# Lightning attention and a four-expert layer: the first stretch written as one list of steps, w1 loaded between chunks, values of the third unit at other places

## The chip, the cores and the metric

The kernel runs on one core of a Trainium2 chip. A core has TensorE (PE, matmuls, with its weight loads PEld), VectorE (DVE), ScalarE (ACT), GpSimd (POOL) and SyncE (SP, which issues most DMAs). The metric is the device time of one execution in microseconds (us). The kernel before has a median of 1180.59 us over three runs (1180.34 to 1181.72).

## What is computed

A linear attention with decay over 4 batches, 8 heads, 768 tokens and head size 64 is followed by four experts, all of them applied to every token and mixed by normalised weights. All values are float32. Cut to what matters:

```python
for b in range(nb):                                   # blocks of 64 tokens
    intra = np.einsum('bhic,bhjc->bhij', qb, kb) * Dmask[None]
    intra = np.einsum('bhij,bhjd->bhid', intra, vb)
    inter = np.einsum('bhid,bhde->bhie', qb * lam_pow[None], kv_state)
    out[:, :, sl] = intra + inter
    kv_state = lam_block * kv_state + np.einsum('bhsd,bhse->bhde', kb * rev_pow, vb)
...
p = domain_probs / (domain_probs.sum(-1, keepdims=True) + 1e-09)
for e in range(E):                                    # x is 3072 x 512, w1 512 x 1024, w2 1024 x 512
    h = np.maximum(x @ w1[e], 0.0)
    out += p[:, e:e + 1] * (h @ w2[e])
```

## The kernel before, in words

**Tiling.** A chunk is 128 tokens of one batch, all 8 heads; a batch has 6 chunks (NCH). A group is 8 chunks, 1024 tokens, and there are three groups. The attention's output for a group lies turned in `xT` (L309). A unit is one pair of a group and an expert, 12 in all, numbered from 0.

**Products.** The expert products are made by a scheme of seven products in place of eight (M1 to M7) with sums of operand blocks beforehand: sums S of w1, sums T of x and of w2. Most first products (`first_product`, L883, matmul L905) are nested: each of the seven is itself made of seven, and its operands are four more sums of each side. Second products (`second_product`, L944, matmul L959) use w2's T sums. The product of group 0 with expert 0 is special: it is made straight after the attention by `direct_product` (L1301, matmul L1315), which has four quarters for each of M1 to M7; M6, M7 and M4 add up in banks of their own (`pc` in the profile).

**The first stretch (L1366 to L1410).** The attention of group 0 is three steps a chunk. `turn` (L549) multiplies k by its decay on GpSimd (`kd`, L520), transposes q and k on TensorE into two PSUM banks, and copies them out on ScalarE. `scores` (L572) multiplies q with k, and kd with v; then VectorE masks the scores and adds to the state, `middle` for the second half-block, `end` for the next chunk's state (L605 to L616), whose scaled copy GpSimd makes at L616. `values` (L622) adds the part from the state and the part from the scores, ScalarE copies the result to `xT` (L661), and VectorE adds the rest (L664, emitted one step later through `adds`). A loop over i calls turn of chunk i, scores of i - 1 and values of i - 2, all three on the pair of PSUM banks `pairs[n % 3]`; the table `between` (L1366) puts quarter products of M1, M2 and M5 at given i. In the same loop come w1's sums S1 to S4 of expert 0 on GpSimd (`sum_w1`, L352), the first own sums of x for product M1 of unit 0's nested product (`own_x`, L1217, on VectorE), the T1 sum of x (`x_sums`, L1338), and the loads: chunks 0 to 3 ahead of the loop (L408 to L412), chunk i + 4 at the end of step i, w1's A12, A21 and A22 after i = 0, 1 and 2. A11 is used by M1, A12 by M2, S1 = A21 + A22 by M5, S2 = S1 - A11 by M6, S3 = A11 - A21 by M7 and S4 = A12 - S2 by M3.

**After it** M5, M6, M7, M3 and M4 of that product follow (L1431 to L1446), a quarter at a time, with one background step (`rest`) and one `pump` a quarter. Then come the units, each with seven positions i of eight parts x (L1472 to L1551): a second product of this unit and a first product of the next, in turn.

**What sets the order.** Each engine and SyncE's queue work in program order. A counter `now` goes up by one a step. `pump` (L150) takes at most one item from the list `chores` when `now` has reached `free`, which grows by GpSimd's counted work; chores are the preparation of weights (`prepare_w2`, L242: load B12 and B22, a pause of 4, load B11, then T3, B21 and T1, T2, T4), the raw w1 of expert 1, and that expert's own operand sums (`mine`, L1415). Before a first product the chores are taken at once until its operands are made (L885). SyncE's loads of w2 for a second product (`feed2`, L929) wait for a buffer that an earlier second product frees, and what is queued behind them waits too. `bring_across` (L368) cuts a DRAM-to-DRAM rearrangement of q and k into pieces that `trickle` issues one at a time.

**Attention of the later groups** is cut into 24 steps (`attention`, L666: turn, scores, values of each chunk, always on banks s0 and s1), and one is taken at chosen parts of the units (L1547): at x = 5 of each i, and at x = 2 of i = 1, 3 and 5 except in units 0 and 3.

Of the kernel before, what the change touches and what calls it, by code (L numbers as in the profile page):

```python
# [12 lines left out]
ALU = mybir.AluOpType  # L13
AX = mybir.AxisListType
FP32 = mybir.dt.float32
# [7 lines left out]
def kernel(  # L23
# [384 lines left out]
    for n, names in ((0, "qk"), (1, "qk"), (0, "v"), (2, "qk"), (1, "v"), (3, "qk")):  # L408
        load(n, names)
    raw_w1(0, "A11")  # L410
    load(2, "v")
    load(3, "v")  # L412
# [30 lines left out]
    q_decay = consts.tile([P, NHP, BL], FP32, name="q_decay")  # L443
    for r in range(2):
        nc.vector.tensor_copy(out=q_decay[half[r], :, 0], in_=lam_bc[half[r], 4 * r:4 * r + 4])
    m = 1
    while m < BL:
        nc.vector.tensor_tensor(
            out=q_decay[:, :, m:2 * m], in0=q_decay[:, :, 0:m],
            in1=q_decay[:, :, m - 1:m].to_broadcast([P, NHP, m]), op=ALU.mult,  # L450
        )
        m *= 2
# [77 lines left out]

    def begin_state(n):
        if n % NCH == 0:
            states[n] = small("kv")[:].rearrange("p (x h d) -> p x h d", x=2, d=D)
            nc.vector.memset(states[n][:, 0], 0.0)

# [36 lines left out]
    def scores(n, tags):  # L572
# [3 lines left out]
        qT, kT = turned[n][0:2]  # L576
        kd, vn = nat.pop((n, "kd")), nat[n, "v"]
# [34 lines left out]
        def end():  # L612
            s = states[n + 1] = small("kv")[:].rearrange("p (x h d) -> p x h d", x=2, d=D)
            passed(nc.vector, s[:, 0], states[n][:, 1])
            tt(nc.vector, s[:, 0], s[:, 0], added[1], ALU.add)
            passed(nc.gpsimd, s[:, 1], s[:, 0])  # L616
# [48 lines left out]

    def attention(g):  # L666
# [21 lines left out]
        return steps  # L688
# [528 lines left out]
    def own_x(m, at_once=False):  # L1217
# [49 lines left out]
        late.append((now[0] + 8, lambda: (ready(), keep())))  # L1267
# [90 lines left out]
    def quarter_5(x):  # L1358
# [7 lines left out]
    between = {  # L1366
        4: (m1[0], m1[2]), 5: (m2[0], m2[2]), 6: (m1[1],), 7: (m1[3],), 8: (m2[1],),
        9: (m2[3], quarter_5(0), quarter_5(2)),
    }
    for i in range(CPG + 2):  # L1370
        if i == 6:
            chores.extend((*prepare_w2(0), *(raw[n] for n in ("A11", "A22", "A21"))))
        more = list(between.get(i, ()))
        order = [(turn, 0), (scores, 1), (values, 2)]
        if i == 3:
            order[0:2] = order[1::-1]
        for f, lag in order:
            n = i - lag
            if more and lag == 0 and i < CPG:
                more.pop(0)()  # L1380
            if 0 <= n < CPG:
                f(n, pairs[n % 3])
            if i < 2 and lag == 0:
                warm(3 - i)
            if i == 6 and lag == 2:
                sum_w1(0, "S1", "A21", "A22", ALU.add)
                sum_w1(0, "S3", "A11", "A21", ALU.subtract)
                own_blocks["M1"] = own_x("M1", True)
            if i == 7 and lag == 2:
                sum_w1(0, "S2", "S1", "A11", ALU.subtract)  # L1390
                sum_w1(0, "S4", "A12", "S2", ALU.subtract)
            if i == 8 and lag == 0:
                x_sums(("T1", 0))
            if i == 9 and lag == 2:
                x_sums(("T1", 1))
            if more and (lag == 2 or i >= CPG):
                more.pop(0)()
            now[0] += 1
            pump()
        while more:  # L1400
            more.pop(0)()
        if i + 4 < CPG:
            load(i + 4)
        if i < 3:
            for name in (("A12",), ("A21",), ("A22",))[i]:
                raw_w1(0, name)
        if i == 5:
            nc.scalar.dma_start(out=probs[:], in_=moe_domain_probs.rearrange("(t p) e -> p t e", p=P))
# [22 lines left out]
    for m in SEQ0[2:]:  # L1431
# [4 lines left out]
        for x, f in enumerate(work):  # L1436
            f()
            for y in sums_then.get((m, x), ()):
                y()
            rest()  # L1440
# [31 lines left out]
    for at, (g, e) in enumerate(units):  # L1472
# [14 lines left out]
        for i in range(7):  # L1487
# [34 lines left out]
            for x, part in enumerate(order):  # L1522
# [24 lines left out]
                if steps and (at > 0 or i > 1) and (x == 5 or (x == 2 and i in (1, 3, 5) and at not in (0, 3))):  # L1547
                    steps.pop(0)()
# [4 lines left out]
    assert not (background or aside or chores or queue or late or results)  # L1553
# [28 lines left out]
```

## Time and profile before

| what | value |
|---|---|
| median of three runs | 1180.59 us |
| the profiled execution, its span | 1180.84 us, 1179.1 us |
| TensorE busy | 1159.9 us, 98% |
| VectorE, ScalarE, GpSimd busy | 793.6, 272.5, 651.0 us |
| mean granted clock of TensorE | 0.997 |
| DMA | 324.45 MB, mean 275 GB/s |

Busy time is the union of an engine's instructions. A row of the timeline has start, length, engine, line, operation, output and inputs by the program's names, how many instructions were merged, and in brackets the idle time before the first with what ended it. "issue" stands for idle time in which the engine waited for nothing that the profile shows. PE clock 0.50 means that the chip granted half of TensorE's clock. A share of DMA is the mean busy share of 16 DMA engines.

### The profile page before, as it was taken

What the parts mean: (1) busy time and instruction counts of PE and PEld (TensorE: products, weight loads), DVE (VectorE), ACT (ScalarE), POOL (GpSimd) and SP (SyncE); (2) the same over time, 40 slices, a digit from 0 to 9 for tenths busy, and PEclk for the clock granted to TensorE, in tenths of its full rate; (3) what the DMA queues carried; (4) which work ended last, traced back from release to release, by engine and by line L of the source; (5) the groups of instructions that cost most, each with busy time, mean ns of one, the idle gap of its engine ahead of it and who ended that gap; (6) DMA issues with size and microseconds to landing.
All of it is one profiled execution on the core that took longest, in us unless ns stands there. A gap on an engine that the chain in (4) does not pass through costs nothing.

```text
span 1179.1 us, 21213 instructions
## 1 busy us (share of the span) xinstructions
PE 1159.9 (98%) x8159; PEld 1011.2 (86%) x8159; DVE 793.6 (67%) x1417; ACT 272.5 (23%) x500; POOL 651.0 (55%) x624
## 2 busy tenths in 40 slices
PE   7899999999999999999999999999999999999998
PEld 7788888888888888888888888888888888888887
DVE  5686796468467857747856764764665676777785
ACT  2323122112201211311220110121243342341231
POOL 2567348539548910065436655415683683783884
PEclk8999999999999999999999999999999999999999
DMA  8779799999999997899998899898986657566543
GB/s 203 191 238 279 252 298 341 366 324 338 351 363 337 318 292 232 260 312 294 326 306 274 280 308 313 283 321 289 315 283 244 248 199 280 196 251 236 214 165 86
DMA packets 265621, 324.45 MB, mean 275 GB/s; under 512 B 121488, under 2 KB 206896, under 8 KB 265520
## 3 DMA queue, kind: packets, MB, share of 16 engines
q1 hardware_dynamic: 254912, 320.27, 81.9%
q10 hardware_dynamic: 10608, 2.82, 1.1%
q8 instruction: 65, 1.06, 0.4%
q14 instruction: 36, 0.29, 0.1%
HBM read 237.69 MB, written 89.54 MB: 278 GB/s over the span
## 4 chain that ended last, share of the span: by engine, by line
PE 95%; DVE 3%; DMA 1%; SPq 1%; issue 0%; ACT 0%; ACTq 0%; DVEq 0%
PE pg L905 39%; PE q L959 33%; PE pq L1185 13%; PE pM L1315 2%; PE pc L1315 2%; PE op L638 1%; PE sp L585 1%; PE op L654 1%; DVE m L96 1%; PE sp L592 1%; PE qp L561 1%; PE kp L561 1%; DVE sums L96 0%; DMA vn<-in_v_dram 0%; DVE hS L96 0%; SPq L124 0%
## 5 line engine op out<-in xcount | busy, mean ns | idle before, releaser
L905 PE MATMUL pg<-xs_in,ws_in 128*128 128x256 f32 x1960 | 469.8, 380 | 0.3 <-DVE m L96 0.3
L905 PEld LDWEIGHTS pg<-xs_in,ws_in 128*128 128x128 f32 x1960 | 371.2, 190 | 52.2 <-DVE m L96 1.8
L96 DVE TENSOR_TENSOR m<-pg,m 128x512 f32<-128x512 f32 x451 | 307.2, 686 | 99.6 <-PE pg L905 93.2
L959 PE MATMUL q<-w2t,hS 128*128 128x256 f32 x1024 | 243.4, 380 | 0.0
L959 PEld LDWEIGHTS q<-w2t,hS 128*128 128x128 f32 x1024 | 193.2, 190 | 26.5
L975 DVE SCALAR_TENSOR_TENSOR acc<-q,gate,acc 128x256 f32<-128x256 f32 x192 | 92.5, 482 | 160.6 <-PE q L959 160.2
L959 PE MATMUL q<-w2t,m 128*128 128x256 f32 x768 | 182.7, 381 | 0.0
L959 PEld LDWEIGHTS q<-w2t,m 128*128 128x128 f32 x768 | 144.8, 190 | 19.9
L917 ACT ACTIVATE m<-m 128x512 f32<-128x512 f32 x132 | 83.0, 630 | 278.6 <-DVE m L96 277.3
L96 POOL TENSOR_TENSOR m<-m,xT 128x512 f32<-128x512 f32 x64 | 80.6, 1275 | 73.0 <-ACT m L917 55.4
L96 POOL TENSOR_TENSOR kv<-kv,q_decay 128x256 f32<-128x256 f32 x20 | 13.9, 696 | 161.9 <-DVE kv L96 132.9
L96 DVE TENSOR_TENSOR sums<-pq,sums 128x256 f32<-128x256 f32 x153 | 64.1, 421 | 46.1 <-PE pq L1185 38.9
L913 ACT COPY m<-pg 128x512 f32<-128x512 f32 x88 | 51.5, 585 | 172.2 <-PE pg L905 162.8
L1185 PE MATMUL pq<-acc,w2t 128*128 128x256 f32 x352 | 86.6, 379 | 0.0
L1185 PEld LDWEIGHTS pq<-acc,w2t 128*128 128x128 f32 x352 | 66.8, 190 | 9.3 <-issue 0.3
L96 POOL TENSOR_TENSOR acc<-hT,hT 128x512 f32<-128x512 f32 x32 | 40.2, 1271 | 30.3 <-PE pq L1185 28.4
L96 POOL TENSOR_TENSOR w2o<-w2b 128x512 f32<-128x512 f32 x32 | 40.4, 1283 | 26.9 <-DMA w2b<-in_moe_w_dram 25.1
L96 POOL TENSOR_TENSOR ops<-w2b 128x256 f32<-128x256 f32 x24 | 19.2, 820 | 62.1 <-DMA w2b<-in_moe_w_dram 54.7
L848 ACT ACTIVATE m<-m 128x512 f32<-128x512 f32 x44 | 27.7, 630 | 104.5 <-DVE m L96 104.5
L96 DVE TENSOR_TENSOR hS<-m,m 128x512 f32<-128x512 f32 x56 | 46.7, 836 | 5.0 <-ACT m L917 5.0
L96 DVE TENSOR_TENSOR m<-m,m 128x512 f32<-128x512 f32 x56 | 47.0, 839 | 0.0
L96 POOL TENSOR_TENSOR acc<-hT,acc 128x512 f32<-128x512 f32 x32 | 40.7, 1271 | 7.4 <-PE pq L1185 5.4
(165 smaller groups left out, 1376.7 us busy)
## 6 DMA issues: line engine op xcount, KB each, us to landing
xs_in<-x_ops SPq DMA_DIRECT2D x70, 896.0 KB, 6.5
ws_in<-w_ops SPq DMA_DIRECT2D x70, 896.0 KB, 8.5
w2t<-w_ops SPq DMA_DIRECT2D x66, 256.0 KB, 6.8
w2t<-w_sums SPq DMA_DIRECT2D x64, 256.0 KB, 3.9
w_ops<-ops SPq DMA_DIRECT2D x28, 512.0 KB, 5.6
w2t<-in_moe_w_dram SPq DMA_DIRECT2D x48, 256.0 KB, 4.1
w2b<-in_moe_w_dram SPq DMA_DIRECT2D x32, 256.0 KB, 5.8
w_sums<-w2o SPq DMA_DIRECT2D x16, 512.0 KB, 4.6
```

Source lines behind the costliest of these rows:

```text
L96: eng.tensor_tensor(out=o, in0=a, in1=b, op=op)
L561: nc.tensor.transpose(out=x[:, ac * C:(ac + 1) * C], in_=y[:, 2 * ac:2 * ac + 2].rearrange("p r d -> p (r d)"), identity=ident[:],)
L585: nc.tensor.matmul(out=sp[r][half[x], ac * BL:(ac + 1) * BL], lhsT=hc(kT)[half[r], ac, blk[x]], rhs=hc(qT)[half[r], ac, blk[x]], start=(ac ...
L592: nc.tensor.matmul(out=sp[x][half[r], 256 + ac * D:256 + (ac + 1) * D], lhsT=kd[half[x], 2 * ac + r], rhs=vn[half[x], 4 * r + ac], start=F ...
L848: nc.scalar.activation(out=o[:], in_=o[:], func=AF.Relu)
L905: nc.tensor.matmul(out=p[:, j * 256:(j + 1) * 256], lhsT=ws[i][:, j * P:(j + 1) * P], rhs=xs[i], start=(fresh and j == 0), stop=True, skip ...
L913: nc.scalar.copy(out=new[at][:], in_=p[:])
L917: nc.scalar.activation(out=new[at][:], in_=new[at][:], func=AF.Relu)
L959: nc.tensor.matmul(out=p[:, s * DH:(s + 1) * DH], lhsT=h[A_OF[m]][:, c * 256 + s * P:c * 256 + (s + 1) * P], rhs=fed2[g, e, m][uu][:, c], ...
L975: nc.vector.scalar_tensor_tensor(out=o, in0=x, scalar=w, in1=o, op0=ALU.mult, op1=ALU.add)
L1185: nc.tensor.matmul(out=p[:, 0:256], lhsT=fed3[e, m, x // 2][:, x % 2, c * P:(c + 1) * P], rhs=b[B_OF[i]][:, c * 256:(c + 1) * 256], start= ...
L1315: nc.tensor.matmul(out=p[:, s * 256:(s + 1) * 256], lhsT=a[c][:, f:f + P], rhs=b[:, c, j * 256:(j + 1) * 256], start=(s == 0 and c == 0 an ...
```

## The change

1. The loads ahead of the loop become q and k of chunks 0 and 1, v of 0 and 1, w1's A11, chunk 2, A12, chunk 3. The others follow in steps 3 to 6: chunks 4 and 5, 6, 7, and then A21 and A22.
2. `q_decay` is made by four scans over the block instead of six doubling products.
3. The scaled copy of the state that GpSimd makes moves from the end of `scores` into `begin_state`, which `turn` and now `scores` call: it is issued at the next chunk's turn, or at its scores if these were issued before the state was there.
4. The loop over i becomes a list of 34 steps. PSUM pairs are taken in turn by every call, not by chunk. The order from chunk 2 on has a quarter product between the scores and the values of most chunks.
5. S1 is issued with turn 7, S2 with the last quarter of M2, S3 behind M5's second remaining quarter, S4 behind M6's first. The own x sums of M1 are no longer made in the first stretch but by the chore `mine["M1"]`. The chores begin at step 30.
6. `m1[4]()` and `m2[4]()` are called twice. The first has no effect for M1; the second sets up M2's hidden block and appends its five background steps, so these are made twice.
7. The steps of the later attention have their places written out. For group 1, units 0 and 1 keep theirs; in the third unit turn and scores keep theirs too, and values move from (i, x) = (1, 5), (3, 5) and (5, 5) to (2, 2), (4, 2) and (6, 2). For group 2 nothing moves.

```diff
-    for n, names in ((0, "qk"), (1, "qk"), (0, "v"), (2, "qk"), (1, "v"), (3, "qk")):
+    for n, names in ((0, "qk"), (1, "qk"), (0, "v"), (1, "v")):
         load(n, names)
     raw_w1(0, "A11")
-    load(2, "v")
-    load(3, "v")
+    load(2)
+    raw_w1(0, "A12")
+    load(3)
...
+    lam_q = consts.tile([P, NHP], FP32, name="lam_q")
     for r in range(2):
-        nc.vector.tensor_copy(out=q_decay[half[r], :, 0], in_=lam_bc[half[r], 4 * r:4 * r + 4])
-    m = 1
-    while m < BL:
-        nc.vector.tensor_tensor(
...
+        nc.vector.tensor_copy(out=lam_q[half[r]], in_=lam_bc[half[r], 4 * r:4 * r + 4])
+    for ac in range(NHP):
+        nc.vector.tensor_tensor_scan(
...
     def begin_state(n):
-        if n % NCH == 0:
+        if n % NCH == 0 and n not in states:
...
+        if n % NCH and n in states and n not in carried:
+            carried.add(n)
+            passed(nc.gpsimd, states[n][:, 1], states[n][:, 0])
...
         qT, kT = turned[n][0:2]
+        begin_state(n)
...
-            passed(nc.gpsimd, s[:, 1], s[:, 0])
...
+    FEW = tuple((i, 5) for i in range(7))
+    MANY = (0, 5), (1, 2), (1, 5), (2, 5), (3, 2), (3, 5), (4, 5), (5, 2), (5, 5), (6, 5)
+    WIDE = (0, 5), (1, 2), (2, 2), (2, 5), (3, 2), (4, 2), (4, 5), (5, 2), (6, 2)
...
+    PLACES = {1: places(u0=FEW[2:], u1=MANY, u2=WIDE), 2: places(u3=FEW, u4=MANY, u5=MANY[:7])}
...
-    for i in range(CPG + 2):
...
+    pair = itertools.cycle(pairs)
+
+    def attend(f, n):
+        return lambda: f(n, next(pair))
+
+    ts, ss, vs = ([attend(f, n) for n in range(CPG)] for f in (turn, scores, values))
...
+    for f in (
+        (ts[0], lambda: warm(3)), (ts[1], lambda: warm(2)), (ss[0], loads(4, 5)), (ss[1], loads(6)), (vs[0], loads(7)),
+        (vs[1], loads("A21", "A22")), (ts[2],), (m1[0],), (ss[2],), (m1[2],), (vs[2],), (ts[3],), (m2[0],), (ss[3],), (m2[2],),
+        (ts[4],), (vs[3],), (ss[4],), (ts[5],), (m1[1],), (vs[4],), (ss[5],), (ts[6],), (m1[3],), (vs[5],), (ss[6],),
+        (ts[7], sum_first("S1", "A21", "A22", ALU.add), load_probs), (m2[1],), (vs[6], sum_x(0)), (begin_chores, ss[7]),
+        (m2[3], sum_first("S2", "S1", "A11")), (vs[7],), (quarter_5(0),), (sum_x(1), quarter_5(2)),
+    ):
+        for work in f:
+            work()
+        now[0] += 1
+        pump()
+    later_sums = {("M5", 1): sum_first("S3", "A11", "A21"), ("M6", 0): sum_first("S4", "A12", "S2")}
+    m1[4]()
+    m2[4]()
     m1[4]()
     m2[4]()
...
+            if (m, x) in later_sums:
+                later_sums.pop((m, x))()
...
-                if steps and (at > 0 or i > 1) and (x == 5 or (x == 2 and i in (1, 3, 5) and at not in (0, 3))):
-                    steps.pop(0)()
+                if steps and steps[0][0] == (at * 7 + i, x):
+                    steps.pop(0)[1]()
```

More of the change, by code (lines that the diff above doesn't have):

```diff
@@ L443 @@
     q_decay = consts.tile([P, NHP, BL], FP32, name="q_decay")
+    lam_q = consts.tile([P, NHP], FP32, name="lam_q")
     for r in range(2):
-        nc.vector.tensor_copy(out=q_decay[half[r], :, 0], in_=lam_bc[half[r], 4 * r:4 * r + 4])
-    m = 1
-    while m < BL:
-        nc.vector.tensor_tensor(
-            out=q_decay[:, :, m:2 * m], in0=q_decay[:, :, 0:m],
-            in1=q_decay[:, :, m - 1:m].to_broadcast([P, NHP, m]), op=ALU.mult,
+        nc.vector.tensor_copy(out=lam_q[half[r]], in_=lam_bc[half[r], 4 * r:4 * r + 4])
+    for ac in range(NHP):
+        nc.vector.tensor_tensor_scan(
+            out=q_decay[:, ac], data0=lam_q[:, ac:ac + 1].to_broadcast([P, BL]), data1=zeros[:, 0:BL],
+            initial=1.0, op0=ALU.mult, op1=ALU.add,
         )
-        m *= 2
     states = {}
@@ L529, in decayed @@
         tt(nc.gpsimd, *(x.rearrange("p (ac r) d -> p ac r d", r=2) for x in (kd, kn)), by, ALU.mult)
+    carried = set()
     def begin_state(n):
-        if n % NCH == 0:
+        if n % NCH == 0 and n not in states:
             states[n] = small("kv")[:].rearrange("p (x h d) -> p x h d", x=2, d=D)
             nc.vector.memset(states[n][:, 0], 0.0)
+        if n % NCH and n in states and n not in carried:
+            carried.add(n)
+            passed(nc.gpsimd, states[n][:, 1], states[n][:, 0])
     def turn_across(n):
@@ L664, in values, with places @@
             adds.append((now[0], lambda o=o, p=p: tt(nc.vector, o, o, p, ALU.add)))
+    FEW = tuple((i, 5) for i in range(7))
+    MANY = (0, 5), (1, 2), (1, 5), (2, 5), (3, 2), (3, 5), (4, 5), (5, 2), (5, 5), (6, 5)
+    WIDE = (0, 5), (1, 2), (2, 2), (2, 5), (3, 2), (4, 2), (4, 5), (5, 2), (6, 2)
+    def places(**units):
+        return [(int(at[1:]) * 7 + i, x) for at, of in units.items() for i, x in of]
+    PLACES = {1: places(u0=FEW[2:], u1=MANY, u2=WIDE), 2: places(u3=FEW, u4=MANY, u5=MANY[:7])}
     def attention(g):
@@ L687, in attention @@
             steps.append(end)
-        return steps
+        return list(zip(PLACES[g], steps, strict=True))
     hid = {}
@@ L1215, with own_x @@
     to_do, own_sums = {}, []
-    def own_x(m, at_once=False):
+    def own_x(m, at_once=False, wait=8):
         name = B_OF[m]
@@ L1266, in own_x @@
         keep = keep_own(("x", 0, m), x_ops[0, MS.index(m)], pieces)
-        late.append((now[0] + 8, lambda: (ready(), keep())))
+        late.append((now[0] + wait, lambda: (ready(), keep())))
         return {i: b[B_OF[i]] for i in B_OF}
@@ L1364, in quarter_5 @@
         return step
[L1366 to L1369, printed above, removed]
-    for i in range(CPG + 2):
[L1371 to L1408, printed above, removed]
@@ new lines, with sum_first, begin_chores, load_probs @@
+    pair = itertools.cycle(pairs)
+    def attend(f, n):
+        return lambda: f(n, next(pair))
+    ts, ss, vs = ([attend(f, n) for n in range(CPG)] for f in (turn, scores, values))
+    def sum_first(name, a, b, op=ALU.subtract):
+        return lambda: sum_w1(0, name, a, b, op)
+    def begin_chores():
+        chores.extend((*prepare_w2(0), *(raw[n] for n in ("A11", "A22", "A21"))))
+    def load_probs():
+        nc.scalar.dma_start(out=probs[:], in_=moe_domain_probs.rearrange("(t p) e -> p t e", p=P))
@@ new lines, in loads, with sum_x @@
+    def loads(*of):
+        return lambda: [raw_w1(0, x) if isinstance(x, str) else load(x) for x in of]
+    def sum_x(i):
+        return lambda: x_sums(("T1", i))
+    for f in (
[9 more added lines that the diff above has]
+        pump()
@@ L1552 @@
     pump(force=True)
-    assert not (background or aside or chores or queue or late or results)
+    assert not (later_sums or background or aside or chores or queue or late or results)
 _INS = ['q', 'k', 'v', 'lam', 'moe_domain_probs', 'moe_w1', 'moe_w2']
```

## The prediction, made before the change was run

> **What bounds the kernel now.** I read the busy table first, then the windows, then the timeline of TensorE, then its waits, then SyncE's and GpSimd's timelines where the moved steps meet them. The first line of the page settles what can be won:
>
> ```profile
> PE 1159.9 (98%) x8159; PEld 1011.2 (86%) x8159; DVE 793.6 (67%) x1417; ACT 272.5 (23%) x500; POOL 651.0 (55%) x624
> ```
>
> The span is 1179.1 us, so TensorE is idle for 19.2 us in all; the change removes none of its work, so it can win idle time and slow clock only. Where they lie is told by the windows (us of the span, then busy time of PE, PEld, DVE, ACT, POOL, granted clock, DMA share, GB/s):
>
> ```profile
> 5.70:16.42 10.72, 8.72 (x258) 7.75 (x258) 9.83 (x26) 4.38 (x9) 4.79 (x5) 1.00 1.07 246
> 16.42:23.25 6.83, 4.72 (x104) 4.30 (x104) 2.53 (x6) 1.17 (x2) 1.49 (x2) 0.50 0.80 191
> 23.25:41.40 18.15, 15.57 (x326) 13.49 (x320) 8.07 (x21) 6.31 (x14) 6.67 (x8) 1.00 0.91 221
> 41.40:66.20 24.80, 22.14 (x504) 18.55 (x502) 17.68 (x36) 8.08 (x18) 18.74 (x16) 1.00 0.55 159
> 66.20:94.00 27.80, 27.78 (x129) 24.46 (x130) 23.19 (x36) 10.20 (x18) 16.85 (x15) 1.00 0.90 268
> ```
>
> Up to 66.2, where product M6 starts (the `pc` rows), idle time is 2.00 + 2.11 + 2.58 + 2.66 = 9.35 us, and half of the 4.72 us at clock 0.50, 2.36 us, is lost too: **11.7 us** in reach there. TensorE's timeline (start, length, what, count, idle before and its releaser) has the causes:
>
> ```profile
> 14.31 0.62 PE L654 MATMUL op<-st,vn 64*64 64x64 f32 x27 [0.91 <-issue]
> 18.53 1.13 PE L592 MATMUL sp<-vn,kd 64*64 64x64 f32 x32 [3.07 <-DMA vn<-in_v_dram]
> 24.74 1.96 PE L1315 MATMUL pM<-xT,w1b 128*128 128x256 f32 x8 [1.31 <-ACT xT L661]
> 39.34 1.97 PE L1315 MATMUL pM<-xT,w1b 128*128 128x256 f32 x8 [1.27 <-DVE xT L96]
> 47.81 0.63 PE L561 MATMUL qp<-ident,qn 128*128 128x128 f32 x4 [1.69 <-issue]
> 62.09 3.69 PE L1315 MATMUL pM<-xt,w1o 128*128 128x256 f32 x16 [0.55 <-DVE xt L96]
> ```
>
> The longest is chunk 2's v, which stands behind w1's A11 and chunk 3's q and k; two are quarter products put directly behind the values they need. Later there are three idle times of 1.31 us, one per chunk of the third unit:
>
> ```profile
> 320.01 0.62 PE L638 MATMUL op<-qs,kv 64*64 64x64 f32 x26 [1.31 <-DVE kv L96]
> ```
>
> The others stand at 350.12 and 380.22: **3.93 us**. There values come three parts after scores and reuse the banks s0 and s1, which the state update still reads: the last DVE add (kv from sp, 379.75 to 380.17 for the third) ends just before TensorE goes on.
>
> [...] here these loads run at 191 to 246 GB/s, while 200 to 250 us shows 351. [...]
>
> **The order of the loads.** In KB from the start, v of chunk 2 ended at 3328 and landed at 18.40; it ends at 2816 now. The old landings (2560 KB at 15.08, 3072 at 17.37, 3584 at 20.51, 4096 at 22.58) give about 16.5 for it. In the new list it is due after turn 2 and one quarter, near 18.5: 3.07 goes. Chunk 3's k ends at 3840 KB, about 21.5, and is due at 22.3; A12 (3328, 18.4) is due at 23.3. w1's A21 and A22 now come last (8192 KB, landed at 41.36 before) and are used by GpSimd for S1. All these loads are new tiles, so SyncE should not wait for buffers. Cost nothing; if DMA is 1 us later, 0.2 to 1 us of it shows at turn 3.
>
> **The list of steps.** The same matmuls run. One by one from the old spacings, a turn takes 0.97 us, scores 0.98, values 1.05, a quarter 1.85. Old work from 5.69 to 66.22 is 60.53 - 11.7 = 48.8 us. What idles in the new list: (a) chunk 1's values need chunk 0's last state add, the GpSimd scaling (1.0) and a further DVE add: DVE 0.74 + 0.41 + 0.42 + 0.42 after the scores, then GpSimd, then 0.41; values 1 starts near 13.9 and TensorE idles 1.7. (b) Scores 4 follow turn 4 by one step only, and turn 4's ACT copies (0.59 each) queue behind the Relu of the quarter before, which waits for its DVE add (0.69): 0.8. (c) M6 behind the T2 sum: 0.44 as now. (d) Blocks of instructions: 2.60 now; the steps are spread more evenly, but follow one another faster; no row bounds it, so 0 to 2.6, taken as 1.0. Sum 3.9. M6 starts at 5.69 + 48.8 + 3.9 = 58.4 instead of 66.2: **-7.8**. The clock is taken as full: in the window from 13.0 to 16.4 TensorE is then busy some 60%, before 46%, and the window with the 1.27 us wait (63%) was not slowed. If it is slowed, 2.4 comes back. A quarter between scores and values (1.85) covers mask and state add (0.75 + 0.42); without it those 1.2 would show.
>
> **PSUM pairs in turn.** A pair is needed again three or more steps later, over 3 us, against ACT copies 0.65 and DVE adds 0.48: nothing. **q_decay**: six products with 2.96 us become four scans of 0.2 (eight took 1.57): DVE has q scaled 2 us sooner, hidden behind (a).
>
> **GpSimd's scaled state** moves from scores to the next turn, ahead of that chunk's kd. After scores: DVE 2.0, scaling 0.62, kd 1.06, together 3.7; TensorE has quarter, turn, values and half the next scores, 4.3: covered by 0.6. Behind turn 7 stand S1 and S2: about 46.7 + 2 x 2.7 = 52.1; the M5 quarters need S1 from 51. Just covered; each us later costs a us.
>
> **What moves behind M5 and M6.** S3 (2.7) and S4 (2.7) queue before T1, T2 of w2; S3 ends near 55, M7 needs it at 65. M1's own x sums leave DVE (44.69 to 47.3, 2.55 us) and come back as four subtractions (about 3.4) at unit 0's top, covered by the raw first block and the 1.73 us part ahead: 0.3. m2's end is called twice: the four S sums (0.67) and three ACT copies (0.58) of one hidden block are made twice, 2.7 us of DVE in M6 and M7. DVE has 0.44 us of gap per quarter after 80; M3's third quarter waits for its bank: 0.3.
>
> **The chores come later, and their DMAs.** They begin at slot 30 of 34 where it was 19 of 30, and w2's first pause ends in M5, not before. By the planner's count, the second expert's B21 load is issued two parts before product M5's operands are due; before, in unit 0's first part. Now (us, GpSimd, then SyncE):
>
> ```profile
> 99.91 2.50 POOL L96 TENSOR_TENSOR w2o<-w2b,w2o 128x512 f32<-128x512 f32 x2 [4.92 <-DMA w2b<-in_moe_w_dram]
> 102.48 1.41 POOL L96 TENSOR_TENSOR ops<-w1o 128x256 f32<-128x256 f32 x2
> ```
>
> ```profile
> 95.07 1.33 SPq L248 DMA_DIRECT2D w2b<-in_moe_w_dram  x2
> ```
>
> M5's first needed sum is ready at 103.2, TensorE needs it at 109.5: slack 6.3. GpSimd's chain S1, S2, S3, T3, S4, T1, T2 ends at 65.5 instead of 67.2, and the raw loads behind T2's store move by only -1.7; three more across transfers (0.8 each) stand ahead of B21: 95.7 issued, 100.5 landed, T4 2.5, first sum at 103.8. TensorE needs it at 58.4 + 27.7 (M6 to unit 0, as from 66.2 to 93.9) + 12.96 (one product pair, 7 x 0.86 + 4 x 1.73) + 2.6 (one part and a raw block) = 101.7: **+2.1**, between 0 and 5.
>
> **Third unit.** Values move from three to eight parts behind their scores; one part is 1.73 us: -3.93. What is late next: the sums of x for the third group begin 7.3 us later relative to the unit's end. M5's operand sums then end near 397.5, where their store stood at 396.7: about 0.8 of the slack is used, nothing shown.
>
> **Sum**: -7.8 - 3.9 + 0.3 + 0.3 + 2.1 = -9.0. The profiled execution took 1180.84 (span 1179.1 plus 1.74 around it), 0.25 above the median 1180.59. 1180.84 - 9.0 = 1171.8, for a median **1171.6**.
>
> **Rivals.** (B) Unit 0 doesn't wait and instruction blocks come in time: 1171.6 - 2.1 - 1.0 = 1168.5. For: SyncE's gates still hold slack. (C) The clock is halved again or blocks come late twice: + 2.4 to 3: 1174.3. For: the first chunks still leave 1.7 us of idle time. Against: no wait of 3 us is left. (D) The third unit's wait only changes its releaser: 1171.6 + 3.9 = 1175.5. Against: 5 parts, 8.6 us, for 1.31. (E) **Slower**: GpSimd falls behind at unit 0. Its products M5, M6 and M2 then each wait for a T or S sum (2.6) and four operand sums (3.0): 5.6 x 3 = 16.8 instead of 2.1, 1186.3. It decides from the point where GpSimd's first M5 sum comes some 12 us after 101.7. Against: GpSimd idles 6.7 us at 83 to 90 now. (F) The gain of the list is given back to the same DMA-bound start of the units, so that nothing moves: 1180.6.
>
> **Chances.** Forecast 0.45 (1169 to 1173.5), B 0.18, C 0.14, D 0.08, E 0.08, F 0.05, others faster 0.02. The range takes in B, C and D: 1167 to 1176.5. Faster by over 0.2% 0.87, the same 0.05, slower 0.08; 0.2%, 2.4 us, is about what a measurement of this kernel tells from no change.
>
> **What would show it.** M6 (`pc`) starting at 57 to 60 with clock 1.00 throughout; the 3.07 gone; a wait of about 1.7 near 13; none before `op<-qs,kv` around 310 to 380; a wait of some 2 us before `pg<-xt,ops` or `pg<-...w1o` near 101. It is wrong if M6 starts after 62, if S1 or S2 releases the M5 or M6 quarters, or if unit 0 shows waits on GpSimd in more than one product.

## The result and the profile after

The changed kernel takes **1187.45 us** (median of 6 runs, 1183.31 to 1187.85) against 1180.83 for the kernel before in the same comparison: a ratio of 1.0047, with a 95% interval of 1.0031 to 1.0063. It is slower by some 5.5 us by the ratio, and the medians lie 6.6 apart; 1171.6 was forecast. Its profiled execution took 1184.67 us (span 1182.8), 2.8 below its median; what the other runs lose beyond it, no profile shows.

TensorE's busy time rose by 3.1 us with the same number of matmuls, which is a first sign of lost clock:

```profile
PE 1163.0 (98%) x8159; PEld 1011.3 (86%) x8159; DVE 803.6 (68%) x1419; ACT 274.1 (23%) x503; POOL 648.5 (55%) x624
```

The windows of the changed kernel (us of the span, then busy time of PE, PEld, DVE, ACT, POOL, granted clock, DMA share, GB/s) show where: in 15.47 to 18.89 and in 411.42 to 418.25.

```profile
12.06:15.47 3.41, 1.38 (x75) 1.26 (x78) 2.69 (x7) 0.00 (x0) 1.09 (x2) 1.00 1.16 217
15.47:18.89 3.42, 3.42 (x75) 3.30 (x67) 0.97 (x4) 1.84 (x5) 1.20 (x2) 0.50 1.04 255
18.89:41.40 22.51, 22.01 (x513) 19.01 (x512) 13.04 (x32) 9.64 (x21) 6.22 (x7) 1.00 0.89 207
41.40:61.73 20.33, 18.37 (x380) 14.99 (x378) 12.55 (x26) 5.75 (x13) 14.81 (x12) 1.00 0.45 126
61.73:90.94 29.21, 28.11 (x129) 24.23 (x130) 26.62 (x40) 11.63 (x21) 17.72 (x15) 1.00 0.82 237
...
200.00:330.00 130.00, 130.00 (x1125) 112.59 (x1124) 83.46 (x142) 24.97 (x47) 76.21 (x77) 1.00 1.00 343
330.00:407.00 77.00, 75.75 (x584) 65.61 (x583) 63.02 (x104) 13.07 (x23) 59.52 (x60) 1.00 0.98 334
...
411.42:418.25 6.83, 6.07 (x14) 4.88 (x15) 0.00 (x0) 1.17 (x2) 6.44 (x9) 0.50 1.04 299
```

TensorE's timeline of the changed kernel, cut to rows ahead of which it idled (the bracket), and one row of the third unit:

```profile
15.01 0.50 PE L659 MATMUL op<-st,vn 64*64 64x64 f32 x17 [2.01 <-issue]
...
57.59 3.69 PE L1329 MATMUL pM<-xt,w1o 128*128 128x256 f32 x16 [0.58 <-DVE xt L96]
...
61.73 1.53 PE L1329 MATMUL pc<-xt,w1o 128*128 128x256 f32 x6 [0.44 <-DVE xt L96]
...
80.33 1.99 PE L1329 MATMUL pM<-xT,w1o 128*128 128x256 f32 x8 [1.10 <-DVE m L96]
...
107.50 1.13 PE L919 MATMUL pg<-xt,ops 128*128 128x256 f32 x4 [0.86 <-POOL ops L96]
...
138.21 1.10 PE L919 MATMUL pg<-ops 128*128 128x256 f32 x4 [0.96 <-DVE m L96]
...
164.50 1.13 PE L919 MATMUL pg<-xT,w1o 128*128 128x256 f32 x4 [1.02 <-DVE m L96]
...
326.77 0.69 PE L643 MATMUL op<-qs,kv 64*64 64x64 f32 x32
...
353.11 1.10 PE L919 MATMUL pg<-xs_in,ws_in 128*128 128x256 f32 x4 [1.25 <-DMA ws_in<-w_ops]
...
412.18 1.19 PE L919 MATMUL pg<-xs_in,ws_in 128*128 128x256 f32 x2 [3.17 <-DMA ws_in<-w_ops]
```

The wait of 3.07 for chunk 2's v is gone, and so are the three of 1.31: the row at 326.77 has no bracket. M6 (`pc`) starts at 61.73, not at 66.22. But waits stand now in units 0 and 1, and two for `ws_in`, the loaded operands of w1, later. A sum closes the account. The first `pg` matmul (`pg` is the bank of the nested first products, so this is where the units begin) starts at 92.66, where it was 95.65 (-2.99). Idle time after it is 8.17 us, where it was 4.88 (+3.29), and 6.83 us at half clock cost 3.41. Together +3.7, and the span grew from 1179.1 to 1182.8. (Without idle time and lost clock, the stretch from the first `pg` to the last matmul is 1074 to 1075 us in both, and within 1 us of that in nearly every run below.)

The chain of waits that ends at 412.18, in the changed kernel (start, length, what):

```profile
396.98 1.73 POOL xo L96
398.71 0.45 SPq L183
...
400.31 4.74 DMA x_ops<-xo
...
405.12 0.32 SPq L832
...
405.49 6.56 DMA ws_in<-w_ops
412.05 0.14 issue
412.18 1.19 PE pg L919 x2
```

GpSimd's sum of x, its store, the load of it and the load of `ws_in` behind that in SyncE's queue stand one behind another. In the kernel before, the same chain at that place holds matmuls only:

```profile
409.19 0.86 PE pg L905 x4
410.06 1.73 PE q L959 x8
411.78 1.29 PE pg L905 x6
```

There its load landed at 410.64 and was used at 411.62: 0.98 us to spare. That number was to be had before the prediction, and wasn't looked up.

### The profile page after: what moved, and what is told of

It is laid out like the page before. It is cut to its first block, busy times and chain, and to the rows that moved or that the text cites. A ratio compares the mean times of both kernels' runs of the same rounds, so it can differ in the third digit from the quotient of the medians.

```text
span 1182.8 us, 21229 instructions
## 1 busy us (share of the span) xinstructions
PE 1163.0 (98%) x8159; PEld 1011.3 (86%) x8159; DVE 803.6 (68%) x1419; ACT 274.1 (23%) x503; POOL 648.5 (55%) x624
## 2 busy tenths in 40 slices
DMA packets 265621, 324.45 MB, mean 274 GB/s; under 512 B 121488, under 2 KB 206896, under 8 KB 265520
## 3 DMA queue, kind: packets, MB, share of 16 engines
q8 instruction: 65, 1.06, 0.4%
## 4 chain that ended last, share of the span: by engine, by line
PE 88%; DVE 4%; DMA 4%; POOL 1%; issue 1%; SPq 1%; ACT 0%; ACTq 0%; DVEq 0%; POOLq 0%
PE pg L919 37%; PE q L973 30%; PE pq L1199 13%; PE pM L1329 2%; DMA ws_in<-w_ops 1%; DVE m L96 1%; PE op L643 1%; PE sp L591 1%; PE op L659 1%; PE sp L598 1%; DVE hS L96 1%; PE qp L566 1%; PE kp L566 1%; DVE xt L96 1%; PE pc L1329 1%
## 5 line engine op out<-in xcount | busy, mean ns | idle before, releaser
L96 DVE TENSOR_TENSOR m<-m,m 128x512 f32<-128x512 f32 x56 | 49.4, 882 | 0.0
L96 POOL TENSOR_TENSOR ops<-w1b 128x256 f32<-128x256 f32 x24 | 19.3, 823 | 43.4 <-PE pg L919 22.6
```

What stands on the lines that cost most here:

```text
L96: eng.tensor_tensor(out=o, in0=a, in1=b, op=op)
```

## The parts one by one

**The third unit alone.** The kernel before with the places of the third unit's values changed:

```diff
-if steps and (at > 0 or i > 1) and (x == 5 or (x == 2 and i in (1, 3, 5) and at not in (0, 3))):
+if steps and (at > 0 or i > 1) and (
+    x == 5 and not (at == 2 and i % 2)
+    or (x == 2 and i in (1, 3, 5) and at not in (0, 3)) or (x == 2 and i in (2, 4, 6) and at == 2)
+):
```

> The kernel before with one part of the change alone: values of the third unit at (2,2), (4,2), (6,2). Theory 1 (the later values themselves make the x sums of the third group late, and with them the first loads of the fourth unit): the three waits of 1.31 us go, but a wait of 2 us or more on xs_in or ws_in appears near 407 and TensorE's clock may be halved behind it, so 1179 to 1183 us, no gain. Theory 2 (the late chores of the new list are the cause, the values are harmless): 1180.8 - 3.9 = 1176.9 us, no wait near 407.

Measured 1178.2, ratio 0.9983 (0.9971 to 0.9994): about 2.0 of the 3.93 us, between what the two theories gave. The three waits are gone and none stands near 409, so later values by themselves don't make that wait. But two small ones came up behind them:

```profile
436.33 0.89 PE L905 MATMUL pg<-xs_in,ws_in 128*128 128x256 f32 x3 [0.62 <-DVE acc L975]
...
449.88 1.96 PE L905 MATMUL pg<-xs_in,ws_in 128*128 128x256 f32 x8 [0.36 <-DMA ws_in<-w_ops]
```

The first names VectorE, yet its `ws_in` landed at 436.19, 0.13 us ahead of the matmul. The load before 411 also lands 0.13 ahead, at 406.86. So several loads of this kernel land just in time, with nothing to spare.

**The third unit back, in the changed kernel.**

```diff
-PLACES = {1: places(u0=FEW[2:], u1=MANY, u2=WIDE), 2: places(u3=FEW, u4=MANY, u5=MANY[:7])}
+PLACES = {1: places(u0=FEW[2:], u1=MANY, u2=MANY[:9]), 2: places(u3=FEW, u4=MANY, u5=MANY[:7])}
```

> The changed kernel with the third unit's values back at (1,5), (3,5), (5,5). Theory 1: the wait of 3.17 us near 409 and the halved clock behind it (3.4 us) go, three waits of 1.31 us come back: 1187.4 - 6.6 + 3.9 = 1184.7 us, or less where the runs of 1187.4 lose more at that place than the profiled one of 1184.7. Theory 2: the wait near 409 stays, and 3.9 us are added: 1191 us.

Measured 1187.23, ratio 1.0065 (1.0047 to 1.0082), against 1187.45 and 1.0047 (1.0031 to 1.0063). In the profile the waits of 1.31, 1.37 and 1.90 are back and the two for `ws_in` are gone: waiting has moved from one place to another. The third unit's step gains 0.2 us here by the medians and 2.1 by the ratios, whose intervals overlap, so no gain of it is shown inside the changed kernel.

**Chores begun earlier, in the changed kernel.**

```diff
-(ss[5],), (ts[6],), (m1[3],)
+(ss[5],), (begin_chores, ts[6]), (m1[3],)
...
-(begin_chores, ss[7]),
+(ss[7],),
```

> The changed kernel with the chores begun at step 23 of 34 (11 steps ahead of M5's second half, as before) instead of step 30. Theory 2: the operands of units 0 to 3 come earlier, the waits at 106.6 (0.86), 351.9 (1.25) and 409.0 (3.17 and the halved clock, 3.4) go or shrink: 1178 to 1181 us. Theory 1: only the wait at 106.6 goes: 1186 us.

Measured 1181.42, ratio 1.0006 (0.9992 to 1.0019): some 5 us come back (4.8 by the ratios, 6.0 by the medians). No wait is left near 107, 137 and 164. But it is not faster than before, and what waits now is `ws_in`:

```profile
251.65 1.53 PE L919 MATMUL pg<-xs_in,ws_in 128*128 128x256 f32 x6 [2.15 <-DMA ws_in<-w_ops]
...
409.70 1.53 PE L919 MATMUL pg<-xs_in,ws_in 128*128 128x256 f32 x6 [1.00 <-DMA ws_in<-w_ops]
...
454.38 1.12 PE L919 MATMUL pg<-xs_in,ws_in 128*128 128x256 f32 x3 [3.01 <-DMA ws_in<-w_ops]
```

**Late chores alone, in the kernel before.**

```diff
-        if i == 6:
-            chores.extend((*prepare_w2(0), *(raw[n] for n in ("A11", "A22", "A21"))))
...
+            if i == 7 and lag == 1:
+                chores.extend((*prepare_w2(0), *(raw[n] for n in ("A11", "A22", "A21"))))
```

> The kernel before with one edit: the chores begin four steps of the planner later, at the scores of i = 7 and not at the top of i = 6. Nothing else of the change is in it. Theory 1 (it is the later chores that cost the changed kernel its gain): waits for GpSimd's operand sums near 107 to 112 of 0.8 to 2, waits of about 1 for DVE's own x subtractions near 140 and 167, and later ones for ws_in, together 3 to 6 us: 1183.5 to 1187. Rival (the later chores only cost together with the earlier M6, because GpSimd's sums keep their absolute time): M6 stays at 66.2, unit 0 shows at most 0.5 us of new waits, 1180 to 1182.

Measured 1184.39, ratio 1.0033 (1.0022 to 1.0043): +3.9 us from four planner steps (steps of the counter `now`), with M6 at 66.97 where it was 66.22. In the changed kernel the chores begin seven steps nearer to the end of the first stretch than before, so this is the smaller delay. Theory 1 holds in size; of the places that it named only the one near 140 came, with one later wait for `ws_in`, and no wait for GpSimd's sums:

```profile
140.82 1.10 PE L905 MATMUL pg<-ops 128*128 128x256 f32 x4 [0.96 <-DVE m L96]
...
458.02 1.32 PE L905 MATMUL pg<-xs_in,ws_in 128*128 128x256 f32 x5 [2.10 <-DMA ws_in<-w_ops]
```

What a wait on "DVE m" means here is seen in VectorE's timeline of the changed kernel ahead of 138.21: the chore that makes a product's own x sums is forced at the last moment, so four subtractions (the `ops` rows, 3.11 us) stand in one piece ahead of the sums (`m`) that empty the bank TensorE needs.

```profile
133.33 1.82 DVE L96 TENSOR_TENSOR ops<-xT 128x256 f32<-128x256 f32 x2
135.18 1.29 DVE L96 TENSOR_TENSOR ops<-xT,ops 128x256 f32<-128x256 f32 x2
...
136.78 0.68 DVE L96 TENSOR_TENSOR m<-m,m 128x512 f32<-128x512 f32 x1
137.38 1.28 DVE L96 TENSOR_TENSOR m<-pg,m 128x512 f32<-128x512 f32 x2
```

**Ends called once, in the changed kernel** (the second `m1[4]()` and `m2[4]()` deleted).

> The changed kernel with M1's and M2's ends called once each, so that M2's four S sums and three copies are made once. Theory that the doubled sums fill VectorE in M6 and M7: the wait of 1.10 us on VectorE at 79.2 goes, 1186.3 us, and unit 0 starts 1.1 us earlier. Rival (the time is lost at 352 and 409, where DMA is the limit): the 1.10 us are lost again there, 1187.4 us.

Measured 1183.95, ratio 1.0034 (1.0019 to 1.0049). The wait of 1.10 ahead of M3 is gone. That alone says little, since two other profiles with the ends called twice have no such wait over 0.3 either. A steadier measure is the time from M6 to the first `pg`: it is 29.43 us in all 14 profiles with the ends called once, the kernel before among them, and 30.94, 29.72, 30.41, 30.12 and 30.21 in the five with the ends called twice. So the doubled ends cost 0.29 to 1.51 us there. The total fell by more, but the intervals of this run and of the changed kernel overlap, and this run's profile is its longest (1192.91); more is not shown.

**The new order of loads alone, in the kernel before.**

```diff
-for n, names in ((0, "qk"), (1, "qk"), (0, "v"), (2, "qk"), (1, "v"), (3, "qk")):
+for n, names in ((0, "qk"), (1, "qk"), (0, "v"), (1, "v")):
...
-    load(2, "v")
-    load(3, "v")
+    load(2)
+    raw_w1(0, "A12")
+    load(3)
...
-        if i < 3:
-            for name in (("A12",), ("A21",), ("A22",))[i]:
-                raw_w1(0, name)
+        if i == 3:
+            raw_w1(0, "A21")
+            raw_w1(0, "A22")
```

> The kernel before with the new order of loads alone: v of chunk 2 ahead of w1's A12 and of chunk 3's q and k, and A21 and A22 after step 3; everything else is as before. Theory 1 (the 3.07 us wait for v was a matter of the order of the queue): the wait near 18 falls from 3.07 to under 0.8, the clock is not halved after it, so M6 starts 2.5 to 5 us before 66.2, at 61.5 to 63.7, and that gain reaches the end: 1175.5 to 1178.5 against some 1180.7. Theory 2 (the first stretch's loads are short of bandwidth as a whole, and another wait takes the place of this one): M6 at 65 or later, 1180 to 1182. Theory 3 (a gain there is given back by the units, whose loads don't come sooner): M6 at 61.5 to 63.7, but 1180 to 1182, with new waits for ws_in.

Measured 1181.82, ratio 0.9999 (0.9988 to 1.001), M6 at 66.92. Theory 2 holds: the wait for v becomes one for the q that now stands behind it.

```profile
13.36 1.09 PE L562 MATMUL qp<-ident,qn 128*128 128x128 f32 x4 [3.32 <-DMA qn<-in_q_dram]
```

So the new order gains nothing by itself. In the changed kernel the list takes turn 2 only after chunk 0's and 1's values; no run has the list with the old order, so what the order adds there is not shown.

**Four extra matmuls in TensorE's gap, in the changed kernel** (`lambda: warm(4)` ahead of `vs[0]`; their output isn't used).

> The kernel after with four extra matmuls of 128x128 on a constant, some 1.9 us, put in just before chunk 0's values; they fill time in which TensorE idles for 2.01 us by issue, and their output isn't used. Theory 1 (the idle time of that window halves the clock): the granted clock is 1.00 at 15.5 to 19, idle time before chunk 0's values falls by about 1, M6 starts 1.5 to 3 us earlier than 61.73. Rival (the wait is for a block of instructions, which begins at the same count of instructions wherever the idle time is, and the clock is halved by the idle time in sum): the 2.01 wait stays, moves behind the extra matmuls, the clock is still halved, M6 at 61.7 to 63.7. The total follows M6 only if the units don't give it back: 1184.5 to 1186 in the first case, 1187 to 1189 in the second, against 1187.4 of the kernel after.

Measured 1186.76, ratio 1.0044 (1.0029 to 1.0059). What the rival forecast came in this profile: the wait stayed at 1.99, moved behind the extra work, and the clock was halved at 16.3. The rows around the wait tell where it belongs. In the changed kernel it stands behind 14 of chunk 0's second group of matmuls:

```profile
12.57 0.43 PE L659 MATMUL op<-st,vn 64*64 64x64 f32 x14
15.01 0.50 PE L659 MATMUL op<-st,vn 64*64 64x64 f32 x17 [2.01 <-issue]
```

With the extra work, which shows as eight records, it stands eight records earlier in the program:

```profile
13.33 0.29 PE L659 MATMUL op<-st,vn 64*64 64x64 f32 x6
15.61 0.62 PE L659 MATMUL op<-st,vn 64*64 64x64 f32 x26 [1.99 <-issue]
```

In both, 220 matmuls come before it. So in these two profiles it belongs to a count of instructions and not to a place in the program (more on this in the last section). That it is a wait for a block of instructions, as the rival has it, is the author's reading; no row names what TensorE waits for.

One profile is too little for the clock, though. In the five profiles below that have the extra matmuls, this wait is 1.20 to 2.03 us and the clock behind it is not halved; in the five of the list without them it is 2.01 to 2.60 us and the clock is halved each time. So in these ten profiles the clock stayed where TensorE's idle time was filled (1.00 up to 63.22 us in the mended kernel, against 0.97 up to 61.70 in the changed one), as theory 1 had it. M6 starts no earlier for it: at 62.30 to 65.70 with the extra matmuls, at 61.73 to 64.79 without.

## What the mended kernel still waits for

**Early chores, ends once and the extra matmuls together**, with all of the change in it; then the same **with the third unit back** (`u2=MANY[:9]`), so that the list stands without the rest. (The run with early chores has the first, the run with four extra matmuls the last of these edits.)

> The kernel after with three edits together: the chores begin at step 23 as in the run with early chores, the ends of M1 and M2 are called once, and four extra matmuls fill TensorE's idle time before chunk 0's values. Theory 1 (chores, doubled end and halved clock are what the changed kernel lost, and they add up): 1181.4 of early chores, less 1.1 for M3's bank, less 1.5 to 3 for the clock: 1177 to 1179.5. Rival (the loads of the units start no sooner, so what the first stretch wins is waited for at ws_in): M6 at 60 to 62, waits for ws_in of 5 us or more between 200 and 460, 1180.5 to 1182.

> The mended kernel with the third unit's values back at their old places, so that the list of steps stands without the late chores, the doubled ends and the third unit's step; all loads are made. Theory (what the list wins up to unit 0, some 3 us, has only 1.84 us of slack at the fifth load of ws_in before it waits there): a wait of 0.7 to 2.5 near 248, with the clock halved behind it, the three waits of 1.31 are back, 1178.5 to 1182. Rival (the list's gain reaches the end if the third unit's step isn't made, and it was the two together that ran into DMA): no wait for ws_in, 1177 to 1178.

The mended kernel measured 1182.81, ratio 1.0015 (1.0002 to 1.0028), over 22 runs from 1176.72 to 1189.17. The list without the third unit's step: 1184.85, 1.0036 (1.0021 to 1.0051). Repairing what looked broken doesn't make the change win, and the list without the third unit's step is slower than the kernel before by some 4 us. The rival of the first holds (waits for loads of 5.6 in sum, though M6 is later than the 60 to 62 that it gave), and the second is worse than either theory gave. In the mended kernel M6 starts at 63.22 and the first `pg` 3.0 us earlier than before, and then:

```profile
250.34 2.14 PE L919 MATMUL pg<-xs_in,ws_in 128*128 128x256 f32 x7 [2.48 <-DMA ws_in<-w_ops]
...
409.30 1.97 PE L919 MATMUL pg<-xs_in,ws_in 128*128 128x256 f32 x8 [1.18 <-DMA ws_in<-w_ops]
...
438.74 1.53 PE L919 MATMUL pg<-xs_in,ws_in 128*128 128x256 f32 x6 [0.72 <-DMA ws_in<-w_ops]
```

When each `ws_in` landed and when its first matmul started (us; loads counted from the first, from the traces):

```
load        before            third alone       changed           mended
5th         248.77 / 250.61   248.99 / 250.62   248.17 / 251.36   250.25 / 250.34
11th        336.70 / 338.46   330.66 / 336.85   333.85 / 337.46   332.41 / 338.05
16th        410.64 / 411.62   406.86 / 406.99   412.05 / 412.18   409.17 / 409.30
19th        451.97 / 453.05   449.74 / 449.88   455.29 / 456.68   452.97 / 453.11
```

The 5th load lands at 248 to 250 whether TensorE comes early or not. Before, 1.84 us were to spare there and some 1 us at the 16th and 19th. A kernel that comes there 3 us earlier has to wait, unless the load moves too: with the third unit alone the 16th load lands 3.8 us earlier than before, and still only just in time. DMA is the busy resource: its share is 1.00 from 200 to 330 both before and in the changed kernel.

**Bytes or order?** Loads could also be late because of what stands ahead of them in SyncE's queue. To tell the two apart, some loads of `xs_in` (896 KB each) were to be left out. The first attempt, on the kernel before, on the third unit alone and on the mended kernel, left nothing out: its count (`len(fed)`) never took a value at which a load is skipped, and all 70 loads stand in the profiles.

> A control: the kernel before with less to load. Of the first 34 loads of x operands for the nested first products (xs_in) every second one is left out, and the product reads the x operands of the one before it, so its values are not those of the reference; the matmuls, their number and all other transfers stay. 17 transfers of 896 KB go, between 185 and 650 us. Theory (the kernel before waits for DMA nowhere in the units, but its nearest loads of ws_in land only 1 to 2 us ahead of use): nothing changes by more than 1 us, 1180 to 1181.5, while the slack of ws_in at 250 and 411 grows. Rival (DMA holds the kernel before back too): under 1179.

> The kernel before with the third unit's values later, and with the same 17 loads of xs_in left out as in the control (the same products read other x operands). Theory (alone, this step gained 2.5 where it removes 3.93 of waits, since loads of ws_in then land 0.13 us ahead of use): the full 3.9 shows, 1176.5 to 1177.5. Rival (the missing 1.4 has nothing to do with loads): 1178 to 1179.

> The mended kernel (early chores, ends called once, four extra matmuls, with all of the change in it) with the same 17 loads of xs_in left out. Theory (the first stretch's 3 us and the third unit's 3.93 are given back since the loads of the units don't come sooner): with fewer bytes the waits for ws_in at 248, 408, 438 and 452 go, the clock stays at 1.00 there, and the kernel ends some 6 to 7.5 us before its control: 1172.5 to 1175. Rival (the waits come from the planner's order or from GpSimd's sums and not from the DMA engines' bandwidth): waits for ws_in of 3 us or more stay, 1179 to 1183.

They are second samples of kernels that were measured already: before 1181.39, ratio 1.0002 (0.9992 to 1.0011); third unit alone 1179.29, 0.9986 (0.9979 to 0.9992); mended 1181.98, 0.9998 (0.9982 to 1.0013). The intervals overlap those of the first samples, 0.9983 and 1.0015; the expectations were not tried. The two samples of the mended kernel against the 1.0036 of the list without the third unit's step make that step worth 2.5 to 4.5 us there.

The second attempt counts by itself. 53 loads of `xs_in` remain of 70, and 308.86 MB of 324.45; matmuls and all other transfers stay:

```diff
-        xs = stream.tile([P, 7, 256], FP32, name="xs_in", tag="x")
-        nc.sync.dma_start(out=xs[:], in_=x_ops[g, MS.index(m)])
+        feeds[0] += 1
+        if feeds[0] in range(2, 35, 2):
+            xs = last_xs[0]
+        else:
+            xs = stream.tile([P, 7, 256], FP32, name="xs_in", tag="x")
+            nc.sync.dma_start(out=xs[:], in_=x_ops[g, MS.index(m)])
+        last_xs[:] = [xs]
```

> Control: the kernel before with loads of x operands left out by a count of its own: of the first 34 loads of xs_in for nested first products the 2nd, 4th and so on to the 34th, 17 of 896 KB, are not made, and the product reads the x operands of the one before, so its values are not the reference's. Bandwidth theory: the slack of ws_in at 250 and 411 grows by 2 or more, the time stays within 1 us of before, 1179.5 to 1181.5, since nothing waits there. Rival, order: slack and time both as before.

> The third unit's values later and nothing else of the change, with the same 17 loads of xs_in really left out. Bandwidth theory: the whole 3.9 shows against the control, as against some 2.2 with all loads: 1176 to 1177.5. Rival, order: 1178 to 1179.5, with waits for ws_in near 436 and 449 as with all loads.

> The mended kernel (all of the change, early chores, ends called once, four extra matmuls) with the same 17 loads of xs_in really left out. Bandwidth theory: the waits for ws_in at 248, 408, 438 and 452 shrink to under 1 us in sum, the clock stays at 1.00 after 100 us, and it ends 5 to 7 us before its control, 1173 to 1176. Rival, order of SyncE's queue and GpSimd's sums: waits for ws_in of 3 us or more in sum stay, 1179 to 1183.

> The mended kernel with the third unit's values back at their old places, and with the same 17 loads of xs_in left out. Bandwidth theory: no wait for ws_in near 248 (3.8 us with all loads), clock 1.00 there, and the list's 2 to 3 us up to unit 0 reach the end: 1177 to 1179 against 1184.9 with all loads. Rival, order: the wait near 248 stays over 1.5 us, 1181 to 1185.

> The changed kernel as it is (chores from step 30, ends called twice), with the same 17 loads of xs_in left out, so its values are not the reference's. Theory: the waits for ws_in near 352 and 409 (4.4) and the halved clock behind the second (3.4) go, the waits for GpSimd and VectorE near 107, 137 and 163 (2.84) and M3's 1.10 stay: 1187.4 less some 8, 1177.5 to 1180.5. Rival (the late chores' loss lies in their order and not in bandwidth): waits for ws_in of over 2 us stay, 1183 or more.

| kernel | all loads, ratio to before | 17 loads left out, ratio (95%) | median us |
|---|---|---|---|
| before | 1.0002 | 1.0000 (0.9991 to 1.0008) | 1180.68 |
| third unit alone | 0.9983, 0.9986 | 0.9960 (0.9947 to 0.9974) | 1176.63 |
| changed | 1.0047 | 0.9977 (0.9969 to 0.9986) | 1178.35 |
| mended | 1.0015, 0.9998 | 0.9925 (0.9913 to 0.9938) | 1172.32 |
| mended, third unit back | 1.0036 | 1.0002 (0.9991 to 1.0013) | 1181.34 |

By the ratios, the same 17 loads are worth nothing to the kernel before, 2.7 to 3.1 us to the third unit's step alone, 8.3 us to the changed kernel, 8.6 to 10.6 to the mended one, and 4.0 to the list without the third unit's step. What bandwidth theory expected came in four of five, though not in each detail: in the control the slack grew from 0.98 to 3.09 at the 16th load and not at the 5th (1.52), and the mended kernel gained 8.4 on its control, more than the 5 to 7 expected. In the mended kernel with all loads, TensorE's row of windows for 170 to 470 reads

```profile
170.00:470.00 300.00, 294.44 (x2325) 254.41 (x2324) 202.74 (x345) 51.63 (x94) 171.98 (x174) 0.99 0.97 323
```

and with 17 loads left out it is never idle there:

```profile
170.00:470.00 300.00, 300.00 (x2419) 260.64 (x2418) 205.50 (x355) 55.58 (x102) 171.01 (x173) 1.00 0.92 301
```

There the 5th and 16th load of `ws_in` landed at 246.28 and 400.08. In the changed kernel no wait for `ws_in` is left either, while the two on VectorE stay, as expected, since they aren't a matter of loads (that for GpSimd near 107 went, in a profile whose units begin 2.3 us later; M3's is 0.37):

```profile
139.41 0.89 PE L925 MATMUL pg<-ops 128*128 128x256 f32 x3 [0.96 <-DVE m L96]
...
165.71 1.13 PE L925 MATMUL pg<-xT,w1o 128*128 128x256 f32 x4 [1.03 <-DVE m L96]
```

The fifth missed: the list with early chores and fewer bytes has no wait for `ws_in`, as bandwidth theory says, but 1181.34 is not 1177 to 1179. In its profile TensorE waits 2.03 and 3.12 by "issue" in the first stretch, half clock follows the second (mean granted clock of the run 0.998), M6 starts at 65.70, and the three waits of 1.31 have grown to 1.38, 1.60 and 1.87. The mended kernel with fewer bytes has the same first stretch and starts M6 at 62.91. So the list's gain is not a steady 3 us.

Two things stay open. One is how much of that spread comes from the waits named "issue". The other is whether bytes or places in SyncE's queue count, since a load left out saves both. In the mended kernel the 5th `ws_in` was issued at 239.92 and took 10.33 us to land; with fewer loads it was issued at 234.85 and took 11.43, so there the gain is an earlier issue and not a quicker transfer. And the 16th `xs_in`, which in the changed kernel waits for the store of GpSimd's sum and holds `ws_in` up behind it, is itself one of the 17. What is shown is that these loads, by bytes, place or both, take the gains back.

## Why the prediction was wrong, step by step

The step that failed is the sum: gains were carried to the end as if no later load could take them back ("about 0.8 of the slack is used, nothing shown"). The runs showed 0.98 us of slack at the 16th `ws_in` against 6.9 us of gains, and waits for `ws_in` of 4.42 us, with 3.41 lost to the halved clock, in their place. Beside it, the late chores were sized at 2.1 us and cost 4 to 5.

- **What bounds the kernel.** Right that only idle time and slow clock can be won. Missing was the second list: how far ahead of its use each load lands. Rival F ("given back to the same DMA-bound start of the units", chance 0.05) had the mechanism that decided, if not the size.
- **The order of the loads.** Right in effect: 3.07 went in the changed kernel. Alone the new order gains nothing (0.9999).
- **The list of steps**, -7.8, M6 at 58.4. It was -4.5 (61.73), and over eleven profiles with the list M6 stands at 61.73 to 65.70, median 63.2, against 63.10 to 67.22, median 66.2, over seven with the old loop and the old loads: -3.0. Terms (b) and (c) held: 0.50 and 0.44. Term (a), 1.7 ahead of chunk 1's values, did not show: they come right behind the wait of 2.01, and 0.34 stands ahead of chunk 0's. Term (d), 1.0 for the waits named "issue", which were 0.91 + 1.69 = 2.60 before, failed: 2.01 + 0.37 + 0.43 = 2.81 here, and 1.75 + 1.22 + 2.03 = 5.00 in the mended kernel. That they are late blocks of instructions was the author's reading. Two waits of 0.58, one of them the 0.55 of before, were left out. "The clock is taken as full" failed too: the window that was to be busy for some 60% was busy for 40%, half clock followed for 3.42 us, and 1.7 were lost, which rival C had.
- **Doubled end**, 0.3: 1.51 from M6 to the first `pg` in this profile (1.10 of it at M3's bank), 0.29 to 0.98 in four others.
- **PSUM pairs, q_decay, S1 and S2**: no wait names them; right.
- **The chores come later**, +2.1 between 0 and 5. At the place named, M5's sums on GpSimd, 0.86 showed. T4, which reads B21, started at 103.83 where 100.5 was forecast, but M5 asked later too, at 106.64 and not at 101.7:

```profile
96.06 2.50 POOL L96 TENSOR_TENSOR w2o<-w2b 128x512 f32<-128x512 f32 x2 [6.11 <-DMA w2b<-in_moe_w_dram]
...
103.83 2.75 POOL L96 TENSOR_TENSOR w2o<-w2b,w2o 128x512 f32<-128x512 f32 x2 [2.81 <-DMA w2b<-in_moe_w_dram]
106.54 1.78 POOL L96 TENSOR_TENSOR ops<-w1o 128x256 f32<-128x256 f32 x2
```

  But a list that starts late is late at every item: the forced x sums added 0.96 and 1.02, and later stores and loads more. The whole is 3.9 us (four steps, alone) to some 5 (seven steps, undone). This step was sized at its first item only.
- **Third unit**, -3.93, "about 0.8 of the slack is used, nothing shown". The waits went as forecast; that nothing is next failed. The slack was 0.98 at the 16th load, the step was 3.93 and the list 3.0. Alone, 1.7 to 2.0 us arrived at the end; in the changed kernel no gain clear of noise.
- **Sum**, -9.0. It added gains at their places and carried them to the end unpriced. In the changed kernel 6.9 us were gained up to 400, and 10.7 paid: 2.84 in units 0 and 1, 4.42 at `ws_in`, 3.41 by the clock behind it.
- **Rival E** (GpSimd falls behind, slower) had the sign and named the late chores, not the size or engine: the waits were 0.86 to 1.02, not 5.6 each.
- **The signs of being wrong** stayed silent: M6 started at 61.73 and not after 62, neither S1 nor S2 released M5 or M6, and unit 0 waited for GpSimd once. None of them looked at the loads behind unit 0, where the gain was lost.

A version that beats both kernels is the third unit alone, 0.9983 and 0.9986.

## What to carry to other kernels

Before a gain is carried to the end, list for every load behind it when it lands and when it is used; no more than the smallest difference is sure to arrive, unless the load moves too. Where DMA is full (its share was 0.98 to 1.00 from 200 to 407 us here), moving work forward can turn idle time into waiting at a later load, as it did here, and a wait can cost twice: 3.17 us at 412.18, then 3.41 by the halved clock behind it. A background list that starts later is late at all of its items: price it at each one that is forced, not at the first.

## What the runs showed of the hardware

**The halved clock.** In the profiles of the kernel before and of the changed one, the granted clock fell from 1.00 to 0.50 at three places while the products ran. The shortest of the three stays at 0.50 is 3.42 us, so the table has stretches of about that length: one right ahead of each of the three places, and three others that hold a wait named in this document.

| profile, stretch (us) | TensorE busy in it, us | granted clock behind it |
|---|---|---|
| before, 13.01 to 16.42 | 1.55 of 3.41, 45% | 0.50, for 6.83 us |
| changed, 12.06 to 15.47 | 1.38 of 3.41, 40% | 0.50, for 3.42 us |
| changed, 408.00 to 411.42 | 1.02 of 3.42, 30% | 0.50, for 6.83 us |
| before, 36.90 to 40.32 (wait of 1.27) | 2.15 of 3.42, 63% | 1.00 |
| before, 316.80 to 320.21 (wait of 1.31) | 2.10 of 3.41, 62% | 1.00 |
| changed, 349.98 to 353.39 (wait of 1.25) | 2.16 of 3.41, 63% | 1.00 |

In the mended kernel TensorE idled for 1.75 near 14, and the clock stayed at 1.00 up to 60 us. These are single cases, and no limit is drawn from them.

**Waits named "issue".** In the first stretch, with its small matmuls close together, TensorE waits at times for nothing that the profile names: 0.91 and 1.69 us in the kernel before (2.60 in sum), 2.01, 0.37 and 0.43 in the changed one (2.81), 1.75, 1.22 and 2.03 in the mended one (5.00). In the changed kernel they stand behind 450, 1729 and 2241 records of TensorE's queue. The page has a queue of kind "instruction" (q8: 65 packets, 1.06 MB), and each of the five waits of the kernel before and the changed one ended 1.04 to 1.56 us after a packet of it, of 16384 bytes, had arrived (the one at 12.26 took 1.29 us in the changed kernel; TensorE went on at 15.01). That TensorE waits for these packets fits the numbers, but no record says it.

**Eight transfers at a time.** In this program SyncE started no DMA before the one eight places ahead of it had landed: in the kernel before there is no exception in 972, and 90 started within 0.1 us after it; in the changed kernel there is none in 972 either, and 103 started within 0.1 us.
